# Two query tiles per visit to TensorE's halves, filler matmuls in its early gaps, and a reordered start and end

## The chip, the cores and the metric

The kernel runs on one core of one Trainium2 chip. The metric is the device time of one execution in microseconds (us), as the median of three runs: 723.4 us before (722.21 to 724.2). TensorE is called PE here, its weight loads PEld, VectorE DVE, ScalarE ACT, GpSimd POOL, SyncE SP.

## The reference

Local attention with a few global keys, then a two-layer feed-forward block on its output. Batch 4, 8 heads, 768 positions, head size 64; 8 global keys, 96 local ones; the feed-forward block takes 3072 tokens from 512 to 2048 channels and back.

```python
scores = scale * np.matmul(q, k.transpose(0, 1, 3, 2))
scores = scores + bias                      # -slope(head) * distance
scores = np.where(keep, scores, -1000000000.0)   # global or local keys
a = np.exp(scores - np.max(scores, axis=-1, keepdims=True))
a = a / (np.sum(a, axis=-1, keepdims=True) + 1e-09)
x = np.matmul(a, v)                         # heads joined to [3072, 512]
h = x @ w_in
g = np.where(h > 0.0, h, np.exp(np.minimum(h, 0.0)) - 1.0)
out = g @ w_out
```

## The kernel before

The 3072 tokens are 12 groups of 256, each of two q tiles of 128 rows. A group's attention is done for four pairs of heads. Per head and q tile: scores `s` (128 q rows against 232 keys: 96 of the tile before, 8 global, 128 own; in the first group of a batch the first tile has only its own 128), on DVE the bias and the row maximum (line 480, into `pr`), on ACT the exponential with its row sum (line 482), on DVE the inverse of the sum (`inverse`, two small operations on `st`), on ACT or DVE the normalisation (`norm`, line 470 through `scaled`), on PE the transposes `t`, a copy to `pt`, and on PE the product with the values, `pv`. The result is split into a high and a low half, `xh` and `xl`, and the feed-forward block uses three matmuls for a product (high by high, high by low, low by high). It runs over 16 chunks of 128 channels: `h` (line 606, 12 matmuls of 256 columns for a group and chunk), the activation on ACT and DVE, `gh` and `gl`, and `o` (line 628, 6 matmuls of 512 columns).

The weights come as 64-bit floats. Each of the 32 weight tiles (`w_in` and `w_out`, 16 chunks) is loaded as `bits` and turned into its two halves by ACT and five DVE operations of 512 columns (lines 368 to 376, and 295 for the low half). So the first three groups run their feed-forward in three segments (chunks 0 to 4, 5 to 9, 10 to 15), while the weights are still being turned; from the fourth on a group runs through all 16.

The first four groups (`rows` in `EARLY`) do attention in plain 32-bit floats. There the two heads of a pair lie in the two halves of the 128 rows of PE, and `heads32` (line 505) is called for one q tile of one pair: one visit for the scores (two heads side by side, two records of each matmul in the trace), one for four transposes, one for the values. The other eight groups use another function (`head`, lines 561 to 590), which the change leaves alone. While weights are not in yet, their buffers serve as extra buffers of the early groups (`FIRST`), so the late weight loads wait for these.

The order is written out in advance. `Plan.order` (line 102) is a list scheduler: each operation has a cost per engine, a due time, its readers and writers and named buffers (`SLOTS`); the engine that can start soonest takes the operation that is ready, by due time. What it yields is the fixed order of instructions on every engine. `FREE` (line 63) is the time at which each engine is taken to be free first. `run` (line 726) puts the operations out; `warm` (line 748) puts matmuls on a tile `fill` ahead of a PE operation for which the plan has an idle stretch, if `WARM` is set, which it is not (line 712). At the end every engine reads a flag (`flagged`, line 778) and jumps over a general path that the given sizes don't need.

Of the kernel before, what the change touches and what calls it, by code (L numbers as in the profile page):

```python
# [10 lines left out]
I32 = mybir.dt.int32  # L11
# [44 lines left out]
class Plan:  # L56
# [6 lines left out]
    FREE = {"PE": 7000.0, "ACT": 2500.0, "DVE": 7800.0, "POOL": 3000.0, "SP": 1500.0}  # L63
# [158 lines left out]
def load_scalars(nc, pool, srcs):  # L222
    raw = pool.tile([P, len(srcs), 2], I32, name="n_raw")
    for i, src in enumerate(srcs):
        nc.sync.dma_start(raw[:, i], src.bitcast(I32).rearrange("(o n) -> o n", o=1).broadcast_to([P, 2]))
    return raw
# [14 lines left out]
class Kernel:  # L241
# [153 lines left out]
    def pair(self, b, gi, hp, xh, xl, due, step, X):  # L395
# [11 lines left out]
        loads = [p.add(sp(), lambda e: nc.sync.dma_start(rqv.t, src[:, :nq + VC]), writes=[rqv], due=due - (9000 if rows else 14000), nbytes=P * (nq + VC) * 4)]  # L407
        loads += [p.add(sp(), lambda e: nc.sync.dma_start(rk.t, src[:, nq + VC:]), writes=[rk], due=due - (9000 if rows else 14000), nbytes=P * nk * 4)]
# [3 lines left out]
        if rows:  # L412

            if "pr" in X:
                self.loads += loads
# [3 lines left out]
            for i in range(NT):  # L419
                self.heads32(b, hp, t0, i, q32, k32, v32, rqv, rk, pv, due + (2 * i - 2) * step, X)  # L420
# [3 lines left out]
            if "pr" in X:  # L424
                self.held += [o for v in (rqv, rk) for o in v.readers]
# [46 lines left out]
    def softmax(self, b, h, t, s, pr, st, i, d):  # L472
# [8 lines left out]
            pr.t[:, lo:], s.t[:, lo:], tab, -(2.0 ** -(h + 1)), 3.0e38, ALU.add, ALU.min, nm), [s], [pr], d - 4500)  # L481
# [23 lines left out]
    def heads32(self, b, hp, t0, i, q32, k32, v32, rqv, rk, pv, d, X):  # L505
# [3 lines left out]
        t = t0 + i  # L509
        lo, a0, kr, blocks = self.blocks(t)  # L510
        n, c0 = WN - lo, i * (NG + P) + lo
        rows = [slice(64 * j, 64 * j + 64) for j in range(2)]
        ss = [self.bank("s", "s", [P, WN], X.get("s")) for _ in range(2)]
        prs = [self.sb("pr", "pr", [P, WN], slots=X.get("pr")) for _ in range(2)]
        st = self.sb("st", "st", [P, 3, 2])

        def scores(e):
            for r, s in zip(rows, ss):
                nc.tensor.matmul(s.t[:, lo:], q32()[r, 0, i * P:(i + 1) * P], k32()[r, 0, c0:c0 + n], start=True, stop=True)  # L519

        p.add((("PE", 100 + 2.1 * n, False),), scores, [rqv, rk], ss, d - 5000)
        for j in range(2):
            self.softmax(b, 2 * hp + j, t, ss[j], prs[j], st, j, d + j)
        self.inverse(st, d - 3500)
        for j in range(2):
            self.norm(prs[j], lo, st, j, d - 3000 + j, True)
        tp = self.bank("t", "t", [P, 2, 2, P], X.get("t"))

        def transposes(e):
            for j in range(2):  # L530
                for a in range(a0, 2):
                    nc.tensor.transpose(tp.t[:kr, j, a], prs[j].t[:, blocks[a]], self.ident.t)  # L532

        p.add((("PE", 50 + 220.0 * (2 - a0), False),), transposes, prs, [tp], d - 2500)
        pt = self.sb("pt", "pt", [P, 2, 2, P], slots=X.get("pt"))
        for j in range(2):
            p.add(act((2 - a0) * P, True) + dve((2 - a0) * P), lambda e, j=j: self.copy(e, pt.t[:kr, j, a0:], tp.t[:kr, j, a0:]), [tp], [pt], d - 2000 + j)

        def values(e):
            for a in range(a0, 2):  # L540
                for j in range(2):
                    nc.tensor.matmul(pv.t[rows[j], i], v32()[:kr, 2 * i + a, j], pt.t[:kr, j, a], start=a == a0, stop=a == 1)  # L542
# [427 lines left out]
```

## Time and profile before

| | us |
|---|---|
| median of three runs | 723.4 |
| the profiled execution | 722.83 |
| its span, first to last instruction | 721.0 |
| PE busy | 694.5 (96%) |
| DVE busy | 513.2 (71%) |
| ACT busy | 501.4 (70%) |
| POOL busy | 196.4 (27%) |

Busy time is a union of the recorded stretches of an engine. The chain of waits, followed back from the last instruction, is 87% PE; `h` has 35% of the span and `o` 34%. A matmul's recorded length holds its way through the array, so the step from the start of one entry to the start of the next says what it cost the queue; this is used below.

### The profile page before, as it was taken

The page shows a single profiled execution, that of the slowest core. Times are in us where ns is not written, and L with a number is a line of the kernel's source. Part 1 is how long each engine was busy: PE and PEld are TensorE (multiplying, and loading weights), DVE is VectorE, ACT ScalarE, POOL GpSimd, SP SyncE. Part 2 cuts the span into 40 slices and gives each one's busy share as a digit, 9 for nine tenths or more (in the row PEclk, how much of TensorE's full clock was granted, in tenths as well). Part 3 has the DMA queues.
Part 4 walks back from the last instruction along what each step waited for, and adds up shares of the span by engine and source line. Part 5 has one row for each costly group of instructions (what it writes and reads, how often), then busy time and mean ns, then how long its engine had stood idle before and what let it go on. Part 6 is the DMA issues. An engine that isn't in the chain of part 4 may idle for free.

```text
span 721.0 us, 13774 instructions
## 1 busy us (share of the span) xinstructions
PE 694.5 (96%) x4658; PEld 608.6 (84%) x4658; DVE 513.2 (71%) x1575; ACT 501.4 (70%) x1463; POOL 196.4 (27%) x262
## 2 busy tenths in 40 slices
PE   4799999999999999999999999999999999999995
PEld 3466788888888899889999989999999999989894
DVE  5899899997446886785775885875776886774210
ACT  5788888866556776776777786776776876775442
POOL 1000000000004533433443443343344343333221
PEclk9599999999999999999999999999999999999998
DMA  7532691001113122121322322322312311210001
GB/s 290 207 98 85 259 410 63 23 0 31 64 59 109 51 90 88 55 74 57 102 60 71 101 54 67 97 66 66 110 57 66 112 56 51 80 52 1 30 0 35
DMA packets 22254, 62.18 MB, mean 86 GB/s; under 512 B 2720, under 2 KB 4768, under 8 KB 22176
## 3 DMA queue, kind: packets, MB, share of 16 engines
q1 hardware_dynamic: 22176, 61.22, 25.7%
q8 instruction: 39, 0.64, 0.4%
q14 instruction: 39, 0.32, 0.1%
HBM read 54.92 MB, written 6.29 MB: 85 GB/s over the span
## 4 chain that ended last, share of the span: by engine, by line
PE 87%; DVE 6%; ACT 3%; DMA 2%; issue 1%; SPq 0%; ACTq 0%; DVEq 0%
PE h L606 35%; PE o L628 34%; PE pv L587 4%; PE t L575 4%; PE s L561 3%; PE pv L542 3%; PE s L519 2%; PE t L532 2%; DMA rqv<-in_qkv_dram 2%; ACT pr L482 1%; DVE pr L470 1%; DVE pr L480 1%; DVE pt L295 1%; ACT gh L287 1%; DVE x L461 1%
## 5 line engine op out<-in xcount | busy, mean ns | idle before, releaser
L606 PEld LDWEIGHTS h<-xh,w 128*128 128x128 f32 x1536 | 226.4, 188 | 26.0 <-issue 1.7
L606 PE MATMUL h<-xh,w 128*128 128x256 f32 x1536 | 246.1, 283 | 0.0
L628 PE MATMUL o<-w,gh 128*128 128x512 f32 x768 | 241.5, 400 | 0.9 <-ACT gh L287 0.9
L295 POOL TENSOR_TENSOR gl<-e,gh 128x256 fp32r<-128x256 f32 x147 | 114.0, 775 | 339.9 <-ACT gh L287 313.5
L628 PE MATMUL o<-w,gl 128*128 128x512 f32 x384 | 149.6, 404 | 0.0
L612 ACT ACTIVATE e<-h 128x256 f32<-128x256 f32 x192 | 73.4, 382 | 90.8 <-PE h L606 87.2
L628 PEld LDWEIGHTS o<-w,gh 128*128 128x128 f32 x768 | 124.0, 189 | 9.8 <-ACT gh L287 2.0
L614 DVE SCALAR_TENSOR_TENSOR e<-e,h 128x256 f32<-128x256 f32 x192 | 80.2, 418 | 68.8 <-ACT e L613 64.9
L606 PE MATMUL h<-xl,w 128*128 128x256 f32 x768 | 123.5, 283 | 0.0
L606 PEld LDWEIGHTS h<-xl,w 128*128 128x128 f32 x768 | 112.6, 188 | 8.2 <-issue 1.7
L287 ACT CAST gh<-e 128x256 fp32r<-128x256 f32 x192 | 77.4, 403 | 38.0 <-DVE e L614 36.8
L482 ACT ACTIVATE pr<-pr,nmax 128x232 f32<-128x232 f32 (+1 forms) x192 | 90.3, 471 | 16.2 <-DVE nmax L480 14.9
L480 DVE CUSTOM_DVE_ANT_0 pr<-s,tab 128x232 f32<-128x232 f32 (+1 forms) x192 | 70.6, 377 | 38.7 <-PE s L561 29.2
L613 ACT ACTIVATE e<-e 128x256 f32<-128x256 f32 x192 | 80.5, 419 | 3.9
L628 PEld LDWEIGHTS o<-w,gl 128*128 128x128 f32 x384 | 70.7, 188 | 2.1 <-issue 0.9
L295 DVE TENSOR_TENSOR pt<-t,pt 116x256 fp32r<-116x256 f32 (+1 forms) x128 | 51.4, 402 | 25.9 <-ACT pt L287 25.0
L461 DVE TENSOR_TENSOR x<-pv,x 64x256 f32<-64x256 f32 x128 | 53.8, 420 | 21.6 <-ACT x L287 19.2
L470 DVE TENSOR_SCALAR pr<-pr,st 128x232 f32<-128x232 f32 (+1 forms) x161 | 65.9, 441 | 1.4
L289 POOL CAST vd<-rqv 128x512 fp32r<-128x512 f32 (+1 forms) x32 | 18.7, 584 | 143.5 <-DMA rqv<-in_qkv_dram 143.5
L287 ACT CAST pt<-t 116x256 fp32r<-116x256 f32 (+1 forms) x128 | 45.1, 352 | 17.3 <-PE t L575 16.4
L587 PE MATMUL pv<-pt,vd 116*128 116x256 f32 (+1 forms) x240 | 51.0, 289 | 0.0
L575 PE MATMUL t<-ident,pr 128*116 128x128 f32 (+1 forms) x240 | 47.4, 274 | 1.6 <-DVE pt L295 1.6
(87 smaller groups left out, 839.3 us busy)
## 6 DMA issues: line engine op xcount, KB each, us to landing
rqv<-in_qkv_dram SPq DMA_DIRECT2D x32, 512.0 KB, 3.6
rk<-in_qkv_dram SPq DMA_DIRECT2D x32, 368.0 KB, 3.1
bits<-in_w_in_dram SPq DMA_DIRECT2D x16, 512.0 KB, 9.9
bits<-in_w_out_dram SPq DMA_DIRECT2D x16, 512.0 KB, 10.0
rqv<-in_qkv_dram SPq DMA_DIRECT2D x16, 384.0 KB, 3.2
out_dram<-ob SPq DMA_DIRECT2D x24, 256.0 KB, 2.0
rk<-in_qkv_dram SPq DMA_DIRECT2D x16, 184.0 KB, 3.6
n_raw<-in_n_global_dram SPq DMA_DIRECT2D x1, 1.0 KB, 2.5
```

Of the source, the lines that this page charges most:

```text
L287: self.nc.scalar.copy(out, x)
L295: self.on(e).tensor_tensor(out, x, y, ALU.subtract)
L470: self.nc.vector.tensor_scalar(out, x, sc, None, ALU.mult)
L480: p.add((("DVE", 158 + 1.042 * n, False),), lambda e: nc.vector.tensor_tensor_reduce(pr.t[:, lo:], s.t[:, lo:], tab, -(2.0 ** -(h + 1)), 3 ...
L482: p.add(act(n, extra=200), lambda e: nc.scalar.activation(pr.t[:, lo:], pr.t[:, lo:], AF.Exp, bias=nm, scale=-1.0, accum_out=st.t[:, 0, i: ...
L575: nc.tensor.transpose(tp.t[:kr, a], pr.t[:, blocks[a]], self.ident.t)
L587: nc.tensor.matmul(pv.t[:, i].rearrange("p s w -> p (s w)"), vd.t[:kr, 2 * i + a, j].rearrange("p s d -> p (s d)"), pt.t[:kr, a].rearrange ...
L606: nc.tensor.matmul(h.t, w1.t[:, s, cc * P:(cc + 1) * P], x.t[:, cc], start=n == 0 and cc == 0, stop=n == 2 and cc == self.NCC - 1)
L612: p.add(act(W, True), lambda e: nc.scalar.activation(ex.t, h.t, AF.Relu, scale=-1.0), [h], [ex], d - 8000)
L613: p.add(act(W), lambda e: nc.scalar.activation(ex.t, ex.t, AF.Exp, scale=-1.0), [ex], [ex], d - 8000)
L614: p.add(dve(W), lambda e: nc.vector.scalar_tensor_tensor(ex.t, ex.t, -1.0, h.t, ALU.add, ALU.max), [h, ex], [ex], d - 8000)
L628: nc.tensor.matmul(acc[i].t, g.t[:, i * P:(i + 1) * P], w2.t[:, s], start=fc == f0 and n == 0 and s == HI, stop=fc == f1 - 1 and n == 1)
```

## The change

- Early groups: `heads32` becomes `pair32`, once for a pair. Its scores visit holds both q tiles (four matmuls where there were two), and its values visit both too; the transposes are two visits, each of one head and both tiles. One `inverse` serves the four tiles. `pt` is copied in one piece of 512 columns where both tiles are full.
- The buffers of the early groups grow for this (`pr`, `pt`; chunk 11's weights now wait as well, `LATE`).
- `WARM` is on: `fill` matmuls (128x512) at PE's start and in the planned gaps before the first `h`.
- The first pair's loads: q first, then the keys without the 104 columns that the first tile does not use, then the values without one block; the two scalars are loaded from ACT's queue.
- The last group: chunks 14 and 15 start their `h` one step earlier, on up to four buffers; their `gl` is on DVE alone; chunk 15's six `o` matmuls are three for one q tile and then three for the other; the last copy is cut in two, ACT and DVE.
- The flag is read 11 operations before the end of the order.
- `FREE` is changed for four engines. With it and the new operations the plan is made anew, and the order changes in many places.

```diff
-    FREE = {"PE": 7000.0, "ACT": 2500.0, "DVE": 7800.0, "POOL": 3000.0, "SP": 1500.0}
+    FREE = {"PE": 5000.0, "ACT": 3300.0, "DVE": 5700.0, "POOL": 3000.0, "SP": 700.0}
...
-        nc.sync.dma_start(raw[:, i], ...)
+        nc.scalar.dma_start(raw[:, i], ...)
...
+        if b == gi == hp == 0:
+            vs, ks = slice(nq + P, nq + VC), slice(k0, nk)
+            loads = [p.add(sp(), lambda e: nc.sync.dma_start(rqv.t[:, :nq], src[:, :nq]), ...)]
+            def rest(e):
+                nc.sync.dma_start(rk.t[:, ks], src[:, nq + VC + k0:])
+                nc.sync.dma_start(rqv.t[:, vs], src[:, vs])
...
-    def heads32(self, b, hp, t0, i, q32, k32, v32, rqv, rk, pv, d, X):
+    def pair32(self, b, hp, t0, q32, k32, v32, rqv, rk, pv, due, step, X):
...
+        tiles = [(t0 + i, i * (NG + P)) + self.blocks(t0 + i) for i in range(NT)]
+        ss = [self.bank("s", "s", [P, NT, WN], X.get("s")) for _ in range(2)]
+        prs = [[self.sb("pr", "pr", [P, WN], slots=X.get("pr")) for _ in range(NT)] for _ in range(2)]
+        st = self.sb("st", "st", [P, 3, 2 * NT])
         def scores(e):
+            for i, (t, c0, lo, _, _, _) in enumerate(tiles):
+                for j, r in enumerate(rows):
+                    nc.tensor.matmul(ss[j].t[:, i, lo:], q32()[r, 0, i * P:(i + 1) * P], k32()[r, 0, c0 + lo:c0 + WN], start=True, stop=True)
...
         for j in range(2):
+            tp = self.bank("t", "t", [P, NT, 2, P], X.get("t"))
+            def transposes(e, j=j, tp=tp):
+                for i, (_, _, _, a0, kr, blocks) in enumerate(tiles):
+                    for a in range(a0, 2):
+                        nc.tensor.transpose(tp.t[:kr, i, a], prs[j][i].t[:, blocks[a]], self.ident.t)
...
         def values(e):
+            for i, (_, _, _, a0, kr, _) in enumerate(tiles):
+                for a in range(a0, 2):
+                    for j in range(2):
+                        nc.tensor.matmul(pv.t[rows[j], i], v32()[:kr, 2 * i + a, j], pts[j].t[:kr, i, a], start=a == a0, stop=a == 1)
...
+            if final and fc == NFC - 1:
+                for i in range(NT):
+                    def mm3(e, i=i):
+                        for g, s in ((gh, HI), (gh, LO), (gl, HI)):
+                            nc.tensor.matmul(acc[i].t, g.t[:, i * P:(i + 1) * P], w2.t[:, s], start=False, stop=g is gl)
...
-            up(fc, dues[fc])
+            up(fc, dues[fc] - (step if final and fc >= NFC - 2 else 0.0))
...
+            if final and i == NT - 1:
+                for x, at in enumerate((act(W, True), dve(W))):
+                    half = slice(x * W, x * W + W)
+                    p.add(at, lambda e, i=i, ob=ob, half=half: self.copy(e, ob.t[:, half], acc[i].t[:, half]), ...)
...
-    LATE = 12
+    LATE = 11
...
-    FIRST = {"rqv": ["rqv0", "w015", "w115"], "rk": ["rk0", "w014", "w114"], "pr": ["pr0", "pr1", "pr2", "w013", "w113"],
+    FIRST = {"rqv": ["rqv0", "w015", "w115"], "rk": ["rk0", "w014", "w114"], "pr": ["pr0", "pr1", "pr2", "x0", "w013", "w113", "w012", "w112"],
...
-    WARM = False
+    LAST_H = ["h0", "h1", "s0", "s1"]
+    WARM = True
...
+                if i == len(order) - 11:
+                    self.fv = self.flagged()
```

PE at the start, from the scores of the first group's fourth pair on, before. The names are those of the text; the last part of a row is the shape.

```order
L519 MATMUL s_356<-rk_162,rqv_260 128x128
L519 MATMUL s_357<-rk_162,rqv_260 128x128
L519 MATMUL s_361<-rk_162,rqv_260 128x232
L519 MATMUL s_362<-rk_162,rqv_260 128x232
L519 MATMUL s_384<-rk_192,rqv_314 128x232
L519 MATMUL s_385<-rk_192,rqv_314 128x232
L532 MATMUL t_399<-ident,pr_368 128x128
L532 MATMUL t_399<-ident,pr_370 128x128
L532 MATMUL t_412<-ident,pr_376 116x128 x2
```

PE at the same place now; `none<-fill` are the filler matmuls.

```order
L791 MATMUL none<-fill 128x512 x13
L530 MATMUL s_410<-rk_175,rqv_294 128x128
L530 MATMUL s_411<-rk_175,rqv_294 128x128
L530 MATMUL s_410<-rk_175,rqv_294 128x232
L530 MATMUL s_411<-rk_175,rqv_294 128x232
L791 MATMUL none<-fill 128x512 x7
L530 MATMUL s_442<-rk_186,rqv_340 128x232
```

Fillers stand before and behind this pair's scores: 71 of them in all before the first `h`, 14 of these ahead of everything else and 29 from the first of these rows on. Two pairs of the second group have their scores ahead of the first `h`, where one and a half had before; its transposes come behind it.

PE a little later, between `h` and `o` of the second group's time, before.

```order
L519 MATMUL s_689<-rk_432,rqv_560 128x232
L519 MATMUL s_690<-rk_432,rqv_560 128x232
L542 MATMUL pv_695<-pt_674,rqv_453 64x128 x4
L606 MATMUL h_708<-xh_264,w_96_678 128x256 x4
L532 MATMUL t_716<-ident,pr_676 116x128 x2
L532 MATMUL t_716<-ident,pr_685 116x128 x2
L606 MATMUL h_708<-xh_264,w_96_678 128x256 x4
L628 MATMUL o_563<-w_93_703,gh_671 128x512 x2
L606 MATMUL h_708<-xl_271,w_96_678 128x256 x4
L542 MATMUL pv_695<-pt_729,rqv_453 64x128 x4
```

The like of it now.

```order
L629 MATMUL h_558<-xh_300,w_75_380 128x256 x4
L530 MATMUL s_586<-rk_420,rqv_526 128x232
L530 MATMUL s_587<-rk_420,rqv_526 128x232
L530 MATMUL s_586<-rk_420,rqv_526 128x232
L530 MATMUL s_587<-rk_420,rqv_526 128x232
L629 MATMUL h_558<-xl_308,w_75_380 128x256 x4
L564 MATMUL pv_610<-pt_555,rqv_340 64x128
L564 MATMUL pv_610<-pt_596,rqv_340 64x128
```

A pair's `pv` was two visits of four matmuls, with other work between them; now it is one visit of eight (six more follow the last row). From the first `h` to the end of the early groups there were 21 visits for `s` and 24 for `pv`, and there are 10 and 12.

SP at the end, before.

```order
L653 DMA out_dram<-ob_9718 128x512
L653 DMA out_dram<-ob_9720 128x512
L779 TENSOR_LOAD flagint
L902 COMPARE_AND_BRANCH
```

SP at the end now.

```order
L818 TENSOR_LOAD flagint
L688 DMA out_dram<-ob_9704 128x512
L688 DMA out_dram<-ob_9707 128x512
L941 COMPARE_AND_BRANCH
```

The read of the flag has moved ahead of the last two stores; on PE it now stands 8 `o` matmuls before the end, on ACT before the last two copies.

## Rows read from the trace of the kernel before

**Rows 1.** The page: granted clock of PE in 40 slices of the span, in tenths.

```profile
PEclk9599999999999999999999999999999999999998
```

**Rows 2.** Busy time by stretch: length, PE, PEld, DVE, ACT, POOL, clock, DMA, GB/s.

```profile
25.00:30.00 5.00, 3.60 (x20) 2.21 (x19) 4.38 (x17) 3.06 (x9) 0.00 (x0) 0.50 0.45 148
60.00:70.00 10.00, 9.08 (x70) 6.91 (x66) 9.89 (x34) 7.88 (x24) 0.00 (x0) 1.00 0.29 88
120.00:140.00 20.00, 20.00 (x133) 17.23 (x132) 19.48 (x59) 16.24 (x46) 0.74 (x1) 1.00 0.11 30
```

**Rows 3.** Timeline of PE, start: start, length, operation, shapes, count, idle before.

```profile
7.29 3.53 PE L519 MATMUL s<-rk,rqv 64*128 64x128 f32 x16 [7.29 <-ACT rqv L468]
...
13.22 1.10 PE L532 MATMUL t<-ident,pr 128*116 128x128 f32 x4 [0.69 <-DVE pr L470]
...
27.27 1.57 PE L519 MATMUL s<-rk,rqv 64*128 64x128 f32 x8
...
33.87 1.15 PE L519 MATMUL s<-rk,rqv 64*128 64x232 f32 x4
...
38.07 1.67 PE L606 MATMUL h<-xh,w 128*128 128x256 f32 x12
```

**Rows 4.** Timelines of SP's queue and of ACT: the fourth pair's load and scaling.

```profile
17.59 10.14 SPq L407 DMA_DIRECT2D rqv<-in_qkv_dram  x3
...
26.71 0.50 ACT L468 ACTIVATE rqv<-rqv,scale 128x256 f32<-128x256 f32 x1
```

**Rows 5.** Timeline of PE: visits for s and pv between h and o.

```profile
83.75 0.66 PE L519 MATMUL s<-rk,rqv 64*128 64x232 f32 x4
84.34 0.65 PE L532 MATMUL t<-ident,pr 128*116 128x128 f32 x4
...
175.82 1.08 PE L628 MATMUL o<-w,gh 128*128 128x512 f32 x4
176.84 0.44 PE L542 MATMUL pv<-pt,rqv 128*64 128x128 f32 x4
177.21 0.49 PE L628 MATMUL o<-w,gl 128*128 128x512 f32 x1
177.63 0.66 PE L542 MATMUL pv<-pt,rqv 116*64 116x128 f32 x8
178.22 0.50 PE L628 MATMUL o<-w,gl 128*128 128x512 f32 x1
...
179.47 0.61 PE L628 MATMUL o<-w,gh 128*128 128x512 f32 x2
```

**Rows 6.** Timelines of DVE and PE: weights turned and used; DVE's small operations.

```profile
45.72 0.69 DVE L295 TENSOR_TENSOR w<-g,w 128x512 fp32r<-128x512 f32 x1
46.32 0.16 DVE L495 TENSOR_SCALAR st<-st 128x2 f32<-128x2 f32 x1
...
49.36 0.40 DVE L289 COPY pt<-t 116x256 f32<-116x256 f32 x1
49.69 0.33 DVE L470 TENSOR_SCALAR pr<-pr,st 128x232 f32<-128x232 f32 x1
...
170.62 0.69 DVE L295 TENSOR_TENSOR w<-g,w 128x512 fp32r<-128x512 f32 x1 [0.69 <-ACT w L287]
...
46.84 1.21 PE L606 MATMUL h<-xh,w 128*128 128x256 f32 x8
```

**Rows 7.** The end: timeline, the flag's read by SP, and two waits.

```profile
713.13 1.07 ACT L287 COPY ob<-o 128x512 f32<-128x512 f32 x2 [1.52 <-PE o L628]
713.74 1.80 SPq L653 DMA_DIRECT2D out_dram<-ob  x2
...
L779 SPq TENSOR_LOAD <-flagint x1: 515/515/515, 715.6 to 715.6; - x1
...
SPq L902 <- SPq L902: 2.9, 1, 2.9
...
PE s L519 <- DVE nmax L480: 2.0, 3, 0.9
```

More of the change, by code (lines that the diff above doesn't have):

```diff
@@ L224, in load_scalars @@
     for i, src in enumerate(srcs):
[L225 removed]
+        nc.scalar.dma_start(raw[:, i], src.bitcast(I32).rearrange("(o n) -> o n", o=1).broadcast_to([P, 2]))
     return raw
@@ L418, in pair @@
             pv = self.bank("pv", "pv", [P, NT, P], X.get("pv"))
-            for i in range(NT):
-                self.heads32(b, hp, t0, i, q32, k32, v32, rqv, rk, pv, due + (2 * i - 2) * step, X)
+            self.pair32(b, hp, t0, q32, k32, v32, rqv, rk, pv, due, step, X)
             pvs = lambda: pv.t.rearrange("p i w -> p (i w)")
@@ L522, in heads32 @@
+        cost = 250.0 + sum(1.74 * (WN - x[2]) for x in tiles)
+        p.add((("PE", cost, False),), scores, [rqv, rk], ss, d - 5000)
         for j in range(2):
-            self.softmax(b, 2 * hp + j, t, ss[j], prs[j], st, j, d + j)
+            for i in range(NT):
+                self.softmax(b, 2 * hp + j, t0 + i, lambda j=j, i=i: ss[j].t[:, i], ss[j], prs[j][i], st, j * NT + i, d + 2 * j + i)
         self.inverse(st, d - 3500)
+        pts = []
         for j in range(2):
-            self.norm(prs[j], lo, st, j, d - 3000 + j, True)
@@ L527, in heads32 @@
-        tp = self.bank("t", "t", [P, 2, 2, P], X.get("t"))
-        def transposes(e):
-            for j in range(2):
-                for a in range(a0, 2):
[L532 to L542, printed above, removed]
-        p.add((("PE", 140 + 220.0 * (2 - a0), False),), values, [rqv, pt], [pv], d)
-        if "pr" in X:
-            self.held += [o for v in prs + [pt] for o in v.readers]
+            for i, x in enumerate(tiles):
+                self.norm(prs[j][i], x[2], st, j * NT + i, d - 3000 + 2 * j + i, True)
@@ new lines, in pair32 @@
+            tp = self.bank("t", "t", [P, NT, 2, P], X.get("t"))
[3 more added lines that the diff above has]
+                        nc.tensor.transpose(tp.t[:kr, i, a], prs[j][i].t[:, blocks[a]], self.ident.t)
+            n = sum(2 - x[3] for x in tiles)
+            p.add((("PE", 20 + 108.0 * n, False),), transposes, prs[j], [tp], d - 2500 + j)
+            pt = self.sb("pt", "pt", [P, NT, 2, P], slots=X.get("pt"))
@@ L597, in moe @@
         G = {}
+        final = rows + W == self.B * self.S
         def up(fc, d):
             w1 = ws[0][fc]
-            h = self.bank("h", "h", [P, W])
+            h = self.bank("h", "h", [P, W], self.LAST_H if final and fc >= NFC - 3 else None)
             for n in range(3):
@@ L615, in up @@
             p.add(act(W), lambda e: self.copy(e, gh.t, ex.t), [ex], [gh], d - 8000)
-            p.add((dve(W, port=True) if X else ()) + pool(W), lambda e: self.minus(e, gl.t, ex.t, gh.t), [ex, gh], [gl], d - 8000)
+            ends = final and fc >= NFC - 2
+            p.add((dve(W, port=True) if X or ends else ()) + (() if ends else pool(W)), lambda e: self.minus(e, gl.t, ex.t, gh.t), [ex, gh], [gl], d - 8000)
             G[fc] = gh, gl
@@ L647, in moe @@
             ob = self.sb("io", "ob", [P, self.DM])
-            if f0 == 0:
+            if final and i == NT - 1:
+                for x, at in enumerate((act(W, True), dve(W))):
+                    half = slice(x * W, x * W + W)
+                    p.add(at, lambda e, i=i, ob=ob, half=half: self.copy(e, ob.t[:, half], acc[i].t[:, half]), [acc[i]], [ob], end - 9000)
+            elif f0 == 0:
                 p.add(act(self.DM, True), lambda e, i=i, ob=ob: self.copy(e, ob.t, acc[i].t), [acc[i]], [ob], end - 9000)
@@ L900, in tile_kernel @@
             f.run()
-        flag = f.flagged()
+        flag = f.fv
         with tc.If(flag > 0):
```

47 lines of the change are left out of this document (29 added, 18 removed).

## The prediction

> **What bounds the kernel now.** I read the shares of busy time first: PE has 694.5 of 721.0 us, so the question is what PE's own work costs, and where it stands or crawls. The row of the granted clock [rows 1] is full (2.4 GHz) everywhere but in the slice from 18 to 36 us, where it is at half, 1.2 GHz. The table by stretch [rows 2] shows three regimes. From 25 to 30 us PE is at the low level and idle for 1.4 of 5 us, with DVE at 4.38 of 5. From 60 to 70 DVE is at 9.89 of 10 and PE misses 0.9. From 120 to 140 PE has no gap. PE's timeline at the start [rows 3] adds that four transposes cost 1.10 us at 13.22, where at full clock they cost 0.65 (84.34) [rows 5]: PE was slow before the slice that says so, too. The first `h` is at 38.07. From about 71 us on time saved on PE is saved at the end, as long as DVE has the weights in time; before that, DVE must be quicker as well.
>
> **The visits to the halves.** This is the largest term. By start-to-start steps in a stretch at full clock [rows 5]: four `o` and then a `pv` take 1.02 us (175.82 to 176.84), one `o` between two `pv` visits takes 0.42 (177.21 to 177.63). With o the price of one and d what a change to or from the halves adds on each side, 4o + d = 1.02 and o + 2d = 0.42: o is 0.23 and d 0.095. So a visit that stands alone costs 0.19 beside its own time. Its own time: a `pv` of one round 0.37 (176.84 to 177.21), of two rounds 0.59 (177.63 to 178.22): 0.22 a round and 0.15 fixed. Scores of one tile take 0.59 (83.75 to 84.34). How a second tile adds is shown at half clock, where the plan already put two tiles together once: 128 + 232 columns 1.57, 232 alone 1.15 [rows 3], so 0.42 for 128 columns, 3.28 ns a column, 1.64 at full clock. 232 columns are then 0.38 and the fixed part 0.21.
>
> Before, 21 visits for `s` and 24 for `pv` stand between the first `h` and the end of the early groups; now 10 and 12. That is 11 x 0.21 + 12 x 0.15 = 4.1 us of fixed parts, 23 x 0.19 = 4.4 of changes (less 0.3, as four visits stood beside another one before and one does now), and 0.4 for a tile's scores that move ahead of the first `h`; against this one more visit of transposes, 0.4. Together 8.2 us. Bounds: 8.6, and 4.5 if the second tile pays what the rival on weight loads says. Fewer, longer visits cost nothing elsewhere that I can see: the tiles' columns, transposes and exponentials are as many as before.
>
> **The start.** The fourth pair of the first group holds back the first `h`: its load is issued behind the weights at 17.59 and scaled at 26.71 [rows 4]. In the new order the same ten weight loads stand before it, so I leave it there; the two scalar loads that leave SP's queue, the shorter first loads and the earlier first scores bring 1 us at the most. From the scaling to the first `h` PE took 11.4 us, at half clock. What now stands in PE's list from these scores on, at full clock: `s` of 128 + 232 columns 0.80, two more visits of 464 columns 0.97 each, six transposes 1.0 (four are 0.65 at most), a `pv` of three rounds 0.81, and 16 of the fillers. A filler has the shape of an `o`, 0.23, so 3.7 us. With some changes of mode, 8.7 us; from 27.3 the first `h` comes at 36.0, 2.0 sooner. The other 55 fillers stand before that, in waits. The 14 ahead of everything cost 3.2 us at full clock and 6.5 at half, from about 1.5 us on, so they end between 4.7 and 8; the first scores were at 7.29 [rows 3], and at the worst they slip by 0.7, which the wait for the fourth pair's load takes up. Bounds of this term: 4 sooner (the load 1 us early and no wait on DVE), or nothing.
>
> **DVE on the way to the tenth weight.** A weight's last half was done at 46.4 (45.72 + 0.69) and `h` used it at 46.84 [rows 6]: here PE runs on DVE's heels. Counting DVE's instructions up to the tenth weight in both orders: the small operations on `st` go from 34 to 16 (0.16 each; I take 0.2 for the wider ones: 2.4 less), copies to `pt` from 14 to 2 (0.33 from step to step, less for 128 columns; ACT takes them: 3.6 less), normalisations from 17 to 23 (0.33 long, some 0.27 where they overlap the next operation: 1.6 more), `gl`, `xl` and scalings together 0.4 less. 4.8 us less in all. PE's share up to there is 2.0 from the start and 2.8 of the 8.2 (8 and 8 visits become 4 and 4), also 4.8. They keep step, and PE's wait there stays as it is. ACT takes up the copies and gives up normalisations; it comes out even, and has room (7.88 of 10 from 60 to 70 [rows 2]).
>
> Later there is slack: DVE ends the 32nd weight at 171.3 and `o` uses it at 179.47 [rows 5, 6], 8.2 us. PE comes some 10 sooner by then, DVE some 5 (4.4 less work and an earlier start). The slack falls to about 3, for single weights to less. I add 0.5 us of waits; bounds 0 and 3.
>
> **The end.** Behind the last matmul ACT copies two tiles in a row (1.07 from 713.13), SP issues the second store behind the second copy, reads the flag (0.515), jumps, and 2.9 us later goes on [rows 7]. With one tile's six `o` matmuls first, its copy runs beside the other's; the last copy in halves on two engines takes about 0.4. That is 0.65 off the second store. The read ahead of the stores takes 0.5 out of SP's chain. Chunks 14 and 15 earlier close a gap of 0.3 on PE. Against this the read in PE's list, 0.5 long, may open a gap; its queue runs ahead of the array, so I take 0.2. Together 1.25, and I take 1.2; bounds: 0.3 worse (the read in PE's list in full, and the store no sooner), 1.8 better. `gl` on DVE for two chunks is hidden behind `o` either way.
>
> **Sum.** -2.0 - 8.2 + 0.5 - 1.2 = -10.9 us. Of the profiled execution, span 721.0 becomes 710.1, its time 722.83 becomes 711.9. The median of the runs shown, 723.4, stands 0.6 above that execution, so 712.5 us.
>
> **Rivals.** *Weight loads in the open.* A second tile uses the same halves as the first, and its q must be loaded into them: with nothing to hide behind, two passes of 0.186 us (the middle length of the loads at line 519) for each of 10 visits, 3.7 us. That gives 716.2. Against it: the two-tile visit at half clock grew by its columns alone [rows 3], and two rounds of `pv` by 0.22, which 128 columns of four passes fill. For it: at full clock a pass over 232 columns, 0.19, is hardly longer than a load. The Trainium skill (TensorE: Matmul & The Clock Gate, "Part 3: Packing small matmuls — row/col tiling") says that a weight load runs beside matmuls under way only if it goes to another group of rows. By that rule these loads are in the open, and the sum would be 716.2 where rows 3 make it 712.5; no row here shows two tiles in one visit at full clock.
>
> *DVE sets the pace to the tenth weight.* If its 4.8 us turn into waits for ACT (four exponentials now precede each inverse, where two did), nothing is won before 71 us. Of the 23 visits saved 15 come later, 5.3 us, and the end 1.2: 716.9. For it: 9.89 of 10 [rows 2]; against it: the count of instructions.
>
> *PE waits at the head of its queue, and the kernel is slower.* A merged visit needs both `s` banks free of four tiles, and for `pv` both copies; while it waits, every `h` and `o` behind it waits too. Three such waits cost 2.0 us before [rows 7], 0.67 each. If each of the 22 merged visits waited as long, 14.7 us go, and the time is 727.2. It decides from 0.5 us a visit. For it: fixed order; against it: the plan places visits by readiness, and only three of 45 waited.
>
> *Fillers at half clock.* If the level stayed low, the 57 fillers behind the first scores would cost 0.46 each and PE's other work there (four pairs and two score visits by the prices above, some 13) twice as much: the first `h` at about 60, and 736 us. Against it: with the fillers PE has work nearly all the time, and the level was full in every stretch where that was so [rows 2].
>
> *No change to speak of*: what PE saves is lost to a new order that fits the chip less, in many small waits.
>
> **Chances.** Forecast 0.63, with its own range 709.5 to 716; DVE's pace 0.17; weight loads 0.08; waits in the queue 0.06; fillers 0.02; no change 0.04. Faster by over 0.3% (about what runs of this kernel can tell) is the first three, 0.88; within 0.3% 0.04; slower 0.08. The range for 8 in 10 runs from 708 (the better bounds together: 4 + 8.6 + 0 + 1.8 is 14.4, so 709, and 1 for what I don't see) to 719 (DVE's pace with 2 us of further waits).
>
> **What would show it.** Right: the clock's row without a 5 at the start; the first `h` at 34 to 38; PE with 71 instructions more; a score visit of two full tiles at 0.97 and a `pv` of four rounds at 1.03 from start to start; the tenth weight finished on DVE near 65.5; the first `s` of the late groups' function some 10 us sooner; the span's end about 1 us nearer to the end of the last matmul. Wrong: score visits over 1.2 us, waits of over 0.5 us at `s` or `pv`, a clock that falls again before 40 us, or PE idle for over 5 us in all between 40 and 180.

## The result, and the profile after

The changed kernel takes 710.86 us (median of 4 runs, 709.60 to 711.41), the kernel before 723.12 beside it: a ratio of 0.9827, 95% interval 0.9808 to 0.9847. Predicted were 712.5 us, a ratio of 0.985. The profiled execution has a span of 709.3 us (before 721.0) and took 711.11. In a second series at the end of the study the ratio was 0.9849 (0.9819 to 0.9879).

The page's row of PE's granted clock answers to [rows 1]; the slice at half clock is gone.

```profile
PEclk9999999999999999999999999999999999999999
```

Timeline of PE at the start and over the first merged visits (start, length, operation, shapes, count, idle before), the answer to [rows 3, 5]:

```profile
1.36 6.28 PE L791 MATMUL none<-fill 128*128 128x512 f32 x14 [1.36 <-POOL fill L319]
7.57 1.58 PE L530 MATMUL s<-rk,rqv 64*128 64x128 f32 x16
...
26.15 0.89 PE L530 MATMUL s<-rk,rqv 64*128 64x128 f32 x8 [0.27 <-DVE rqv L481]
...
34.58 0.62 PE L629 MATMUL h<-xh,w 128*128 128x256 f32 x3
...
38.81 1.05 PE L530 MATMUL s<-rk,rqv 64*128 64x232 f32 x8
39.80 0.74 PE L629 MATMUL h<-xl,w 128*128 128x256 f32 x4
40.46 1.09 PE L564 MATMUL pv<-pt,rqv 116*64 116x128 f32 x16
41.49 1.19 PE L659 MATMUL o<-w,gh 128*128 128x512 f32 x4
...
62.25 0.63 PE L659 MATMUL o<-w,gh 128*128 128x512 f32 x2
...
206.10 0.27 PE L583 MATMUL s<-ks,qd 128*128 128x232 f32 x1
```

The first 14 fillers take 0.44 us each from 1.36 to 7.57, near twice the 0.23 of a filler at full clock, though the clock's row is full there too; the first scores slip by 0.28. The first `h` is at 34.58, 3.5 us sooner than before. A visit with both tiles' scores takes 0.99 from start to start (38.81 to 39.80), one of four rounds of values 1.03 (40.46 to 41.49): predicted were 0.97 and 1.03. The tenth weight is used at 62.25; before, at 71.34. The first scores of the late groups (the eight that the change leaves alone) come at 206.10; before, at 220.38. The lines of before:

```profile
71.34 1.08 PE L628 MATMUL o<-w,gh 128*128 128x512 f32 x4
...
220.38 0.27 PE L561 MATMUL s<-ks,qd 128*128 128x232 f32 x1
...
711.66 1.20 PE L628 MATMUL o<-w,gh 128*128 128x512 f32 x4 [0.32 <-ACT gh L287]
712.70 0.63 PE L628 MATMUL o<-w,gl 128*128 128x512 f32 x2
```

The tenth weight's last half on DVE, before and after:

```profile
69.76 0.69 DVE L295 TENSOR_TENSOR w<-g,w 128x512 fp32r<-128x512 f32 x1
```

```profile
60.79 0.69 DVE L295 TENSOR_TENSOR w<-g,w 128x512 fp32r<-128x512 f32 x1
```

DVE in three stretches up to the end of the tenth weight (length, DVE busy, clock, DMA share, GB/s), first before and then after:

```profile
8.00:20.00 12.00, 8.78 (x45) 1.00 1.03 405
20.00:38.00 18.00, 16.09 (x62) 0.53 0.52 177
38.00:70.45 32.45, 31.48 (x103) 1.00 0.27 81
sum 62.45, DVE 56.35; mean DVE 18.78
```

```profile
8.00:20.00 12.00, 10.35 (x52) 1.00 1.03 403
20.00:38.00 18.00, 17.77 (x61) 1.00 0.54 187
38.00:61.48 23.48, 22.79 (x75) 1.00 0.34 94
sum 53.48, DVE 50.92; mean DVE 16.97
```

DVE reaches the tenth weight 9.0 us sooner, by 5.4 us less work (56.35 to 50.92) and by 3.5 us less idle time (62.45 - 56.35 = 6.1 to 2.6).

The end (timeline, then SP's stores with their shortest, median and longest time in the queue in ns: after, and before), the answer to [rows 7]:

```profile
702.52 1.06 ACT L287 COPY ob<-o 128x512 f32<-128x512 f32 x2 [1.88 <-PE o L652]
702.79 0.39 PE L652 MATMUL o<-w,gl 128*128 128x512 f32 x1
703.13 1.27 SPq L688 DMA_DIRECT2D out_dram<-ob  x2
703.62 0.42 DVE L289 COPY ob<-o 128x256 f32<-128x256 f32 x1 [2.52 <-ACT ob L287]
```

```profile
L688 SPq DMA_DIRECT2D out_dram<-ob x2: 332/332/332, 703.1 to 704.1; - x2
```

```profile
L653 SPq DMA_DIRECT2D out_dram<-ob x2: 332/822/1311, 713.7 to 714.2; - x2
```

From the end of the last matmul (703.18; before 713.33) to the span's end it is 6.1 us, before 7.6. But DVE's half of the last copy starts when ACT's half ends (702.52 + 1.06 = 703.58), so the copies end 0.86 behind the last matmul as they did before (713.13 + 1.07 = 714.20, 0.87). What went is the read on SP (0.515), with the small step to it 0.56, and 0.98 of the second store: before, it stood 1.31 in SP's queue.

Where the 11.7 us of the span came from:

| stretch | predicted | measured |
|---|---|---|
| up to the first use of the tenth weight | -4.8 (start 2.0, visits 2.8) | -9.1 |
| from there to the end of the last matmul | -5.2 (visits 5.4, gap 0.3, waits +0.5) | -1.1 |
| behind the last matmul | -0.9 | -1.5 |
| sum | -10.9 | -11.7 |

The total was met, its parts were not. The experiments ask why.

### The profile page after: what moved, and what is told of

It is laid out like the page before. It is cut to its first block, busy times and chain, and to the rows that moved or that the text cites. A ratio compares the mean times of both kernels' runs of the same rounds, so it can differ in the third digit from the quotient of the medians.

```text
span 709.3 us, 13861 instructions
## 1 busy us (share of the span) xinstructions
PE 695.9 (98%) x4729; PEld 616.3 (87%) x4729; DVE 508.9 (72%) x1542; ACT 498.1 (70%) x1450; POOL 197.7 (28%) x262
## 4 chain that ended last, share of the span: by engine, by line
PE 77%; DVE 11%; ACT 7%; DMA 2%; issue 2%; SPq 0%; DVEq 0%; ACTq 0%
PE h L629 32%; PE o L659 31%; PE pv L609 4%; PE t L597 3%; PE s L583 3%; ACT pr L493 2%; DMA rqv<-in_qkv_dram 2%; DVE pr L481 2%; DVE e L637 1%; PE pv L564 1%; DVE pt L295 1%; DVE x L472 1%; DVE g L376 1%; DVE pr L491 1%; PE t L547 1%
## 5 line engine op out<-in xcount | busy, mean ns | idle before, releaser
L659 PE MATMUL o<-w,gh 128*128 128x512 f32 x764 | 238.8, 399 | 0.2 <-ACT gh L287 0.2
L659 PE MATMUL o<-w,gl 128*128 128x512 f32 x382 | 147.9, 403 | 0.0
L287 ACT CAST gh<-e 128x256 fp32r<-128x256 f32 x192 | 77.4, 403 | 41.5 <-DVE e L637 40.8
L491 DVE CUSTOM_DVE_ANT_0 pr<-s,tab 128x232 f32<-128x232 f32 (+1 forms) x192 | 69.0, 375 | 33.7 <-PE s L583 31.5
L295 DVE TENSOR_TENSOR pt<-t,pt 116x256 fp32r<-116x256 f32 (+1 forms) x128 | 51.3, 401 | 27.3 <-ACT pt L287 26.4
L481 DVE TENSOR_SCALAR pr<-pr,st 128x232 f32<-128x232 f32 (+1 forms) x172 | 69.6, 445 | 1.4
```

What stands on the lines that cost most here:

```text
L287: self.nc.scalar.copy(out, x)
L295: self.on(e).tensor_tensor(out, x, y, ALU.subtract)
L481: self.nc.vector.tensor_scalar(out, x, sc, None, ALU.mult)
L491: p.add((("DVE", 158 + 1.042 * n, False),), lambda e: nc.vector.tensor_tensor_reduce(pr.t[:, lo:], st_()[:, lo:], tab, -(2.0 ** -(h + 1)), ...
L659: nc.tensor.matmul(acc[i].t, g.t[:, i * P:(i + 1) * P], w2.t[:, s], start=fc == f0 and n == 0 and s == HI, stop=fc == f1 - 1 and n == 1)
```

## The experiments

All are edits of the changed kernel but one, which is built from it by taking the other edits back. Ratios are to the kernel before, run beside them. "Late stretch" is the time from the first scores of the late groups (206.10 in the changed kernel's trace) to the end of the last matmul (703.18): 497.1 there.

**The visits put apart again.**

```diff
-        p.add((("PE", cost, False),), scores, ...)
+            p.add((("PE", 250.0 + 1.74 * (WN - lo), False),), scores, ...)
...
-        p.add((("PE", 150 + 216.0 * n, False),), values, ...)
+            p.add((("PE", 150 + 216.0 * (2 - a0), False),), values, ...)
```

The added lines stand in a loop over the two tiles, with due times apart.

> The changed kernel with the scores and the values of a pair put out again as one operation for each q tile, due apart as before the change; the shared inverse, the transposes by head, buffers, fillers, loads and end stay. From the first h on, 20 visits for scores and 24 for values instead of 10 and 12. Theory (visits cost what the prediction says): 10 x (0.21 fixed + 0.20 for the changes to and from the halves) + 12 x (0.15 + 0.20) = 8.3 us more, 718 to 719.5, with lone score visits of 0.59 and lone values visits of 0.59 from start to start, and h and o beside them 0.09 to 0.11 longer. Rival (PE waits for the weights up to the tenth one, near 62 us, whatever its visits cost): only the visits behind that count, about two thirds: 5.5 us more, 716 to 717. Second rival: the order loses more than the visits (waits at the queue head with another plan), over 720.

717.38 us, ratio 0.9917 (0.9889 to 0.9944), 6.5 more than the changed kernel. Its PE timeline:

```profile
53.35 0.74 PE L628 MATMUL h<-xl,w 128*128 128x256 f32 x4
54.02 0.66 PE L563 MATMUL pv<-pt,rqv 116*64 116x128 f32 x8
54.61 0.73 PE L658 MATMUL o<-w,gh 128*128 128x512 f32 x2
...
55.74 0.66 PE L530 MATMUL s<-rk,rqv 64*128 64x232 f32 x4
56.33 1.21 PE L628 MATMUL h<-xh,w 128*128 128x256 f32 x8
```

Lone visits cost 0.59 each, as before. Summed over the start-to-start steps from the first `h` on, with PE's idle time left out of them:

| us | before | changed | visits apart |
|---|---|---|---|
| steps of `s` | 12.8 | 9.3 | 11.2 |
| steps of `pv` | 13.2 | 11.5 | 13.3 |
| `h` and `o` beside them, above their plain 0.117 and 0.2325 | 7.0 | 3.5 | 6.3 |
| sum | 33.0 | 24.3 | 30.9 |

The 6.6 us of steps are close to the 6.5 us of time; with the idle time the sums are 33.5, 25.3 and 31.4, so 6.1. They are less than the 8.3 expected because many of the visits put apart stand beside transposes or each other: 61 steps of `h` and `o` have such a visit beside them, against 69 before and 35 in the changed kernel. The first rival is not told apart from the theory: the time lies between the two, and the tenth weight is finished at 63.65, 2.2 later than in the changed kernel. The second rival, an order that loses more than the visits, is out.

**The merge alone**: no fillers, old first loads, old `FREE`, old end.

```diff
-    WARM = True
+    WARM = False
-    FREE = {"PE": 5000.0, "ACT": 3300.0, "DVE": 5700.0, ...}
+    FREE = {"PE": 7000.0, "ACT": 2500.0, "DVE": 7800.0, ...}
...
```

> Of the change only the merged visits with their buffers (and the shared inverse, which belongs to them): no fillers, the old first loads, the old free times of the planner, the old end and the flag read last. Theory (the visits are nearly the whole change): the split kernel shows 6.6 us for the visits alone between the first h and the end of the early groups, DVE's 4.8 us less work lets PE have them, and the start and the end bring little without the other edits: 713.5 to 715.5, the tail behind the last matmul 7.6 as before, first h at 36 to 38. Rival (the parts need each other: with PE at half clock to 38 us and the old free times DVE comes no sooner to the tenth weight): 716.5 to 719.

712.56 us, ratio 0.9856 (0.9837 to 0.9876): 1.44 of the 1.73%. First `h` at 36.82, tenth weight at 65.1 (before 70.45), tail 7.3 with a second store of 1.12 (SP's last two stores, shortest, median and longest in ns):

```profile
L684 SPq DMA_DIRECT2D out_dram<-ob x2: 332/726/1120, 705.6 to 706.1; - x2
```

All other edits together bring 0.3%, and 1.2 us of that is the tail; against the second series of the changed kernel (0.9849) they bring 0.1%. The theory holds; the merge, with the shared inverse and DVE's lighter work that belong to it, gave a little more than expected.

**Fillers: none, none with the whole copy, ten more.**

```diff
-    WARM = True
+    WARM = False
```

> The changed kernel without the 71 filler matmuls; the order of everything else is the same. Theory (the clock): the first h came 3.5 us sooner in the changed kernel, 34.58 against 38.07, because PE ran at the full clock from about 9 us on and DVE, which waits for PE's answers there, stood 2.7 us less between 5 and 40 us. Without fillers the row of the granted clock shows a stretch at half clock again before 40 us, the four-transpose and score visits there take about twice as long, the first h is at 36.5 to 38, and the whole kernel takes 2 to 3.5 us more: 713 to 714.5. Rival (the plan): the earlier loads, the new order and DVE's lighter work gave the 3.5 us; fillers stand in waits and cost and give nothing: first h at 34 to 35, 710.3 to 711.3. Second rival: fillers delayed the first scores (7.57 us against 7.29), and without them the time falls below 710.5.

710.27 us, ratio 0.9808 (0.9785 to 0.9831). Its clock row and timeline:

```profile
PEclk9799999999999999999999999999999999999999
```

```profile
36.81 0.62 PE L629 MATMUL h<-xh,w 128*128 128x256 f32 x3
...
62.42 0.69 DVE L295 TENSOR_TENSOR w<-g,w 128x512 fp32r<-128x512 f32 x1
...
208.62 0.27 PE L583 MATMUL s<-ks,qd 128*128 128x232 f32 x1
```

As the clock theory says, the first `h` is 2.2 later, the tenth weight 1.6, the late groups 2.5; but the time is not. The late stretch took 493.7 instead of 497.1. Two kernels were to tell luck from rule. The first has no fillers either, and the last copy whole:

> The changed kernel without fillers and with the last copy whole on ACT: the two single edits that did not lose, together, and a second trace of the order without fillers. Without fillers the first h was 2.2 us later (36.81 against 34.58) and the first scores of the late groups 2.5 later (208.62 against 206.10), yet the last matmul 0.8 sooner: from the late groups' first scores to the last matmul it took 493.7 us, with fillers 497.1, 496.0 and 496.3 in three traces of the same order. Theory A (the late groups lose what the fillers win, whatever the run): 493 to 494.5 us again for this stretch, whole time 709.5 to 710.3. Theory B (that stretch varies by 2 us from run to run, and the trace was a lucky one): 495.5 to 497, whole time 712 to 713.

710.21 us, ratio 0.9827 (0.9810 to 0.9844); late stretch 493.8. The other has ten more fillers right before the first `h`:

```diff
                 if op.n == cold:
+                    self.warm(10 * 240.0, 0.0)
                     self.WARM = False
```

> The changed kernel with ten more fillers right before the first h: 2.3 us of PE's time at that place, nothing else. It asks where the 2.5 us went by which the fillers bring the first scores of the late groups forward. Theory A (the late groups' waits swallow a shift of 2 us): first h near 36.5, the late groups' first scores near 208, the stretch from there to the last matmul near 494 us instead of 496 to 497, whole time as without the ten, 710.4 to 711.2. Theory B (a shift is a shift): the stretch stays at 496 to 497, whole time 712.5 to 713.3.

709.94 us, ratio 0.9821 (0.9802 to 0.9840); first `h` at 37.26, late groups at 207.8, late stretch 495.2. Theory A's time, but a stretch between the two. So 2 us of delay at the first `h` were not seen at the end in any of three kernels.

**The load of the fourth pair moved forward.**

```diff
-    FIRST = {"rqv": ["rqv0", "w015", "w115"], "rk": ["rk0", "w014", "w114"], ...
+    FIRST = {"rqv": ["rqv0", "w015", "w115", "w010"], "rk": ["rk0", "w014", "w114", "w110"], ...
-    LATE = 11
+    LATE = 10
```

> The changed kernel with a fourth buffer for a pair's q and values and for its keys in the early groups (weight chunk 10's places, which then wait too), so that the load of the first group's fourth pair stands behind the first weight instead of behind ten. Theory (the load holds back the first h, as the prediction says): the fourth pair's scores come near 20 us instead of 26.15, the first h 3 to 4 us sooner, near 31, and the whole 1 to 3 us less, 708 to 710. Rival (DVE holds it back: it was busy for 5.00 of 5 us from 20 to 30): the scores come sooner, but the weights come later by as much, the tenth weight is finished at 61 to 62 as now (61.5), and the whole is 710.5 to 712.

709.91 us, ratio 0.9833 (0.9811 to 0.9856). Timeline of PE and DVE:

```profile
26.31 0.62 PE L629 MATMUL h<-xh,w 128*128 128x256 f32 x3
...
61.32 0.69 DVE L295 TENSOR_TENSOR w<-g,w 128x512 fp32r<-128x512 f32 x1 [0.17 <-ACT w L287]
...
206.25 0.27 PE L583 MATMUL s<-ks,qd 128*128 128x232 f32 x1
```

The first `h` is 8.3 us sooner than in the changed kernel, more than either side expected; the new plan also has 23 fillers and two visits for `s` fewer ahead of it, so how much of this is the load stays open. The tenth weight is finished at 62.0 instead of 61.5, the late groups begin at 206.25 instead of 206.10, and the time stays by the ratio (0.9833 and 0.9827; the 709.91 us itself lies in the theory's range, in a series in which the kernel before took 722.58). The rival holds: the first `h` decides nothing. What PE wins there it waits for later. From 20 to 70 us it is idle for 5.8 us, 5.2 of them until something from ACT comes, most of all the normalisation (us in total, times, longest):

```profile
PE t L547 <- ACT pr L479: 2.2, 3, 1.1
```

ACT in turn stands idle for 4.0 us from 20 to 62, 2.2 of them for DVE, and DVE is busy for 40.9 of the 41.5 us from 20 to 61.5. That DVE sets the pace there is argued from these shares.

**DVE's small operations put back.**

```diff
-        self.inverse(st, d - 3500)
+        for i in range(NT):
+            self.inverse(st, d - 3500 + i, i)
```

> The changed kernel with two inverses for a pair, one for each q tile, instead of one for all four: 32 small operations on DVE up to the tenth weight instead of 16, nothing else taken back. Theory A (DVE's lighter work is what lets the merged visits be worth 8.7 us in the early part): 8 pairs of operations at 0.30 from step to step are 2.4 us, the tenth weight is finished at 63.5 to 64 instead of 61.5, and the whole takes 1.5 to 2.4 us more, ratio to before 0.9845 to 0.986. Theory B (such a shift of the early part is swallowed behind 200 us, as in the two kernels without fillers and the one with ten more): tenth weight late by 1.5 to 2.5, ratio 0.981 to 0.9835.

712.05 us, ratio 0.9851 (0.9834 to 0.9867); tenth weight at 64.4, 2.9 later; last matmul 704.92, 1.7 later than in the changed kernel's first trace. This is theory A's ratio, yet the changed kernel's own second series has 0.9849: by the times it stays inconclusive. Nor is the edit the inverses alone: the plan made anew has six copies to `pt` on DVE up to the tenth weight instead of two, and 19 normalisations instead of 23.

**The end: flag last; copy whole; matmuls of the last chunk as before.**

```diff
-                if i == len(order) - 11:
-                    self.fv = self.flagged()
...
-        flag = f.fv
+        flag = f.flagged()
```

> The changed kernel with the flag read behind the last store again. The trace of the changed kernel has 6.1 us from the end of the last matmul to the span's end, the kernel before 7.6. Theory A (as predicted: the read alone): 0.5 us more, 6.6 from the last matmul to the end, the second store's issue 0.33 long. Theory B (the read behind it also made the second store's issue long, 1.31 us instead of 0.33 in the trace of before): 1.5 us more, 7.6 to the end, and the store's issue is 1.3 long although the stores stand 0.94 apart as in the changed kernel. Whole time 711.4 by A, 712.4 by B.

711.34 us, ratio 0.9832 (0.9806 to 0.9858); tail 6.7, the second store 0.33 long at 0.94 behind the first. Theory A: the read is worth 0.56 and does not lengthen the store.

```diff
-            if final and i == NT - 1:
-                for x, at in enumerate((act(W, True), dve(W))):
...
-            elif f0 == 0:
+            if f0 == 0:
                 p.add(act(self.DM, True), lambda e, i=i, ob=ob: self.copy(e, ob.t, acc[i].t), ...)
```

> The changed kernel with the last copy in one piece of 512 columns on ACT, as before the change; the rest stays. Theory (the two halves ran one after the other in the changed kernel: ACT's 703.21 to 703.58, DVE's 703.62 to 704.04): the whole copy takes 0.59 from the end of the last matmul, ends 0.62 behind it instead of 0.86, and the tail is 0.25 us shorter, 5.9; whole time 710.6. Rival (as predicted, halves side by side take 0.4): the tail is 0.2 longer, 6.3. The second store then stands about 0.7 behind the first: if stores that follow each other closely are what makes the issue long (1.31 at 0.49 us distance before), its issue is longer than 0.33.

709.85 us, ratio 0.9806 (0.9780 to 0.9832); timeline:

```profile
702.67 1.28 ACT L287 COPY ob<-o 128x512 f32<-128x512 f32 x2 [1.88 <-PE o L652]
703.28 1.03 SPq L684 DMA_DIRECT2D out_dram<-ob  x2
```

The last matmul ends at 703.32, the copy at 703.95: 0.63 behind it instead of 0.86, tail 6.0. The split was a loss of 0.23 us in the chain; of the time that is too little to see.

```diff
-            if final and fc == NFC - 1:
-                for i in range(NT):
-                    def mm3(e, i=i): ...
```

> The changed kernel with the o matmuls of the last chunk as before the change (high, high, low, low halves tile by tile instead of all three of one tile and then all three of the other); the split copy and the early read of the flag stay. The first tile's copy then starts with the last matmul or after it, as before. Theory (a store issued within 0.5 us of the one ahead of it stands 1.1 to 1.3 us in SP's queue, not 0.33; this, not the copy, was the larger part of the gain behind the last matmul): the two stores stand 0.5 to 0.9 us apart; if they stand under 0.6, the second takes over 1 us and the tail is 6.7 to 7.1; if the halves keep them over 0.65 apart, it takes 0.33 and the tail is 6.4 to 6.6. Rival (prediction's working: only the copy of the first tile, 0.25 to 0.6 us): tail 6.4 to 6.8 with a second store of 0.33 in either case.

711.26 us, ratio 0.9841 (0.9818 to 0.9864); stores 0.73 apart, the second 0.33 long; SP jumps 1.6 behind the last matmul instead of 1.3. The tail is 7.1, because what lies behind SP's jump took 5.5 us here and 4.8 in the changed kernel; the length was not as expected, and that part has 4.6 to 5.5 us in the fourteen traces, whatever the edit. The second store was long in two traces, 1.31 and 1.12, where it stood 0.49 behind the first, and 0.33 in the other twelve, where it stood 0.69 to 0.94 behind. Either edit alone keeps it that far: 0.69 with the copy whole, 0.73 with the matmuls as before.

**Is it POOL that holds the late groups up?** In the changed kernel's trace DVE, POOL and PE at one of the late waits:

```profile
276.39 0.60 DVE L506 TENSOR_SCALAR st<-st 128x2 f32<-128x2 f32 x1
277.02 0.17 DVE L507 RECIPROCAL st<-st 128x2 f32<-128x2 f32 x1
277.22 1.98 DVE L481 TENSOR_SCALAR pr<-pr,st 128x232 f32<-128x232 f32 x2
...
276.35 0.61 POOL L289 CAST vd<-rqv 128x512 fp32r<-128x512 f32 x1 [2.00 <-DMA rqv<-in_qkv_dram]
277.04 1.29 POOL L295 TENSOR_TENSOR vd<-rqv,vd 128x512 fp32r<-128x512 f32 x1
278.28 0.78 POOL L295 TENSOR_TENSOR gl<-e,gh 128x256 fp32r<-128x256 f32 x1
...
278.62 0.40 PE L597 MATMUL t<-ident,pr 128*116 128x128 f32 x2 [0.42 <-DVE pr L481]
```

Two normalisations, 0.33 each when alone, take 1.98 while POOL works, and the transposes wait 0.42.

```diff
-            p.add(..., lambda e: self.minus(e, gl.t, ex.t, gh.t), [ex, gh], [gl], d - 8000)
+            p.add(..., lambda e: e == "POOL" or self.minus(e, gl.t, ex.t, gh.t), [ex, gh], [gl], d - 8000)
...
-                        for g, s in ((gh, HI), (gh, LO)) if n == 0 else ((gl, HI),):
+                        for g, s in ((gh, HI), (gh, LO)) if n == 0 else ((gh, HI),):
```

> The changed kernel without the 146 subtractions for gl that POOL does (0.786 us each, 115 of its 198 us); the o matmuls read gh a second time in their place, so the part of the product that comes from gl is left out, and PE has the same matmuls. It asks why the late groups take 492 to 497 us for the same order. Theory (DVE waits for POOL: the normalisation of 232 columns takes 0.335 us alone and up to 1.46 while POOL works, 37 to 45 of 128 in the late groups, and PE's transposes wait for it): fewer than 25 of them are long, PE's idle time and steps at the late transposes fall by 2 to 4 us, from the late groups' first scores to the last matmul 490 to 494 us, whole time 705 to 708.5, ratio 0.975 to 0.98. Rival (PE waits there for ACT and for its own order; POOL only happens to work at the same time): 495 to 497 us, ratio 0.9815 to 0.984.

709.64 us, ratio 0.9813 (0.9796 to 0.9829); late stretch 495.2. Long normalisations (over 0.5 us) fell from 42 to 18 of 128; each of them, in both traces, overlaps an instruction of POOL. The waits of the late transposes, after and here (us in total, times, longest):

```profile
PE t L597 <- DVE pt L295: 1.2, 4, 0.6
...
PE t L597 <- DVE pr L481: 0.8, 2, 0.4
```

```profile
PE t L597 <- DVE pt L295: 2.8, 3, 1.2
PE t L597 <- DVE pr L481: 0.2, 1, 0.2
```

They did not shrink (2.0 us there, 3.0 here), and most of them ended with another DVE operation. This theory falls: POOL stretches DVE, but taking 146 of POOL's 262 operations away does not give PE the time. What the other 116 cost was not tried.

**The changed kernel again.**

> The changed kernel itself once more, to see what a second trace of it has in the late groups and to set its ratio beside those without fillers (0.9808 and 0.9827) and with ten more (0.9821). Theory A (with fillers PE comes 2 us sooner to the late groups and waits there longer, each time): 495.5 to 497.5 us from the late groups' first scores, near 206, to the last matmul, ratio 0.981 to 0.9835. Theory B (the first trace had bad luck there): 493 to 495 us, span 706 to 708, ratio 0.979 to 0.981.

711.08 us, ratio 0.9849 (0.9819 to 0.9879); trace: late groups at 206.3, late stretch 495.4, span 707.8. Between the two theories. Five traces with the changed kernel's fillers have 495.4 to 497.1 us, two without 493.7 and 493.8, the one with ten more 495.2. One kernel's own scatter is 1.7, so that PE's earlier arrival is what lengthens it is not shown. Two kernels with late arrivals speak against it: the merge alone begins the late groups at 209.8 and takes 495.4, the one with two inverses at 208.9 and 496.0.

No version tried beats the changed kernel by more than the intervals.

## Why the prediction was right, and where it was not

**The visits: right.** Predicted 8.2 us; the steps show 33.0 - 24.3 = 8.7 without PE's idle time (8.2 with it), and `t` with its neighbours the same as before (10.6 and 10.6) in place of 0.4 more. The prices from [rows 2, 3, 5] held to 0.02 us a visit. The merge alone gives five sixths of the gain of the first series, and nearly all of that of the second.

**Weight loads in the open: refuted.** The rival put the two-tile visit at 0.97 + 0.37 = 1.34; it takes 0.99. The second tile's `q` is loaded without a cost that shows. The visit's eight loads stand beside its own matmuls, which run from 38.81 to 39.86:

```profile
38.81 0.69 PEld L530 LDWEIGHTS s<-rk,rqv 64*128 64x128 f32 x8 [0.16 <-DVE rqv L481]
```

The Trainium skill (TensorE: Matmul & The Clock Gate, "Part 3: Packing small matmuls — row/col tiling") says that a weight load runs beside matmuls under way only if it goes to another group of rows. This trace does not agree. Loads and matmuls come in pairs 7 ns apart; if each pair is one for each half of the rows, as I read it, the second tile's loads (from 39.11 on) ran beside matmuls of their own halves.

**The start: the step that failed.** "From 27.3 the first `h` comes at 36.0, 2.0 sooner" went into the sum as 2.0 us. It came 3.5 sooner, 2.2 of it by the fillers (36.81 without them; the merge alone, with the old first loads, has 36.82), and its date is worth nothing that these runs can tell: 8.3 us more (four loads) and 2.2 to 2.7 less (fillers) left the time as it was. In its place stands, as far as the shares of busy time can say, DVE's pace up to the tenth weight, which came 0.5 later when the first `h` came 8.3 sooner. There I counted 4.8 us less work (5.4 came; the small operations in that sum are 2.2 by their own prices, not 2.4) and let PE "keep step"; I did not count DVE's own waits, 6.1 us before and 2.6 after; without fillers, with PE at half clock for part of the time, they are 4.0. So the stretch to the tenth weight gained 9.1 and not 4.8, as the rival "DVE's pace" has it in its mechanism, though not in its sign. On PE's side the 9.1 are the first `h` (3.5), the visits (2.8 by the prices), idle time from the first `h` on (1.9 before, 0.7 after) and 12 `h` that now stand behind the tenth weight (1.4, which is no gain). But this date does not settle the end either: 1.6 to 1.9 later, without fillers and with ten more, it left the time as it was.

**Behind it: the other error.** From the tenth weight on I expected 5.2 us and the first trace has 1.1, the second 2.7. By the prices the visits save 5.7 there (7 for `s` at 0.41, 8 for `pv` at 0.35), and the new order has 1.2 more work behind that point (12 `h` and 4 transposes more, a tile's scores less). The other 1.8 to 3.4 went into waits, for which I had 0.5. Most of them lie ahead of the late groups. From the tenth weight's use to the late groups' first scores it takes 143.9 us in both traces, before 149.0; the visits and 2.3 us less of other work there would make it 141.0. Of these 2.8 us 1.3 are short stops between `h` and `o`, most of them at the same places in both traces. The late groups have 16 `h` and 7 `o` more than before, 3.5 us, and take 4.1 us more in the first trace and 2.5 in the second: 0.6 more waits, or 1.0 less. The cause of the 2.8 is open. So the sum was met because two errors of 4 us cancel. 1.2 to 1.4 of each is one and the same work on the other side of the line; that the rest cancels is luck.

**The end: size right, one price wrong.** Measured 1.5 behind the last matmul, where I had 0.9. The read is worth 0.56 (0.5 predicted). The copy is worth nothing (0.65 predicted): the second half waits for the first. The store's 0.98 I had not seen, since I took [rows 7]'s 1.80 for two stores as given. The read in PE's list opened no gap. The gap of 0.3 that chunks 14 and 15 were to close (0.32 at 711.66 before) is gone.

**The signs.** Met: the clock's row, the first `h`, 71 instructions more on PE, both lengths of visits, PE idle for 1.3 us between 40 and 180, none of it right before an `s` or `pv` visit. Not met: the tenth weight at 61.5 instead of 65.5; the late groups 14.3 us sooner instead of 10, of which 3.5 are `h` and `o` that the new order leaves for later.

## What to carry to other kernels

Price a visit to a part of the array by start-to-start steps at full clock, its fixed part and the change of mode on each side apart; merging visits then gives what the prices say. A milestone of one engine, like the first `h`, belongs in a sum only if nothing else sets the next one: ask which engine arrives last there, and count that engine's waits as well as its work. Two copies that write halves of one tile may run one after the other; look for the second one's releaser before counting them as parallel.

## What the runs showed of the hardware

A change of TensorE between the full array and its halves costs 0.09 us on the matmul ahead (`h` 0.210 instead of 0.117) and 0.106 on the one behind (0.223), before and after alike. A store issued 0.49 us behind another stood 1.1 to 1.3 us in SP's queue instead of 0.33; it was seen twice and not taken apart further. DVE's normalisation of 232 columns takes 0.33 us alone and up to 1.46 while POOL works; the Trainium skill (SBUF — State Buffer, "Who interferes with whom") says that the two share a pair of ports under an exclusive lock, and the fall from 42 long ones to 18 with 146 POOL operations less agrees. One kernel's traces differ by 1.7 us over the same 495 us of one fixed order.
